# Four interleaved attention layers on one core: where rows are normalised, buffers for prepared weights, places of transpositions, and slots for the rest of a second pass

## The chip, the cores and the metric

The kernel runs on one core of a Trainium2 chip. The metric is the device time of one execution in microseconds. A measurement is the median of some runs; one further execution is recorded by the hardware profiler.

## What is computed

Four layers follow each other over 2048 tokens of width 512, in float32: A, B, A, B, with the same weights in both rounds. Each adds to its input what it makes of the normalised input. A is a linear attention with a learned feature map (two softmaxes per head), B an attention within four segments of 512 tokens with a memory carried from segment to segment. There are 32 heads of 16.

```python
def _layernorm(x, axis=-1, eps=1e-5):
    m = jnp.mean(x, axis=axis, keepdims=True)
    v = jnp.var(x, axis=axis, keepdims=True)
    return (x - m) / jnp.sqrt(v + eps)
...
        pq = jnp.einsum("bhsd,hdf->bhsf", q, w_phi)
        pk = jnp.einsum("bhsd,hdf->bhsf", k, w_phi)
        phi_q = jnp.concatenate([_softmax(pq, axis=-1), _softmax(-pq, axis=-1)], axis=-1)
        phi_k = jnp.concatenate([_softmax(pk, axis=-1), _softmax(-pk, axis=-1)], axis=-1)
        kv = jnp.einsum("bhsf,bhsd->bhfd", phi_k, v)
        z  = jnp.einsum("bhsf->bhf", phi_k)
        num = jnp.einsum("bhqf,bhfd->bhqd", phi_q, kv)
        den = jnp.einsum("bhqf,bhf->bhq", phi_q, z)[..., None] + 1e-6
        o = num / den
...
            logits = jnp.einsum("bhqd,bhkd->bhqk", qs, ks) * scale + mask
            p = _softmax(logits, axis=-1)
            a_dot = jnp.einsum("bhqk,bhkd->bhqd", p, vs)
            pq = phi(qs)
            num = jnp.einsum("bhld,bhde->bhle", pq, M)
            den = jnp.einsum("bhld,bhd->bhl", pq, z)[..., None] + 1e-6
            a_mem = num / den
            o = g * a_mem + (1.0 - g) * a_dot
...
    x = A_x
    x = x + _A_ref(_layernorm(x, axis=-1), A_wqkv, A_w_phi, A_wo)
    x = x + _B_ref(_layernorm(x, axis=-1), B_wq, B_wk, B_wv, B_wo, B_beta)
    x = x + _A_ref(_layernorm(x, axis=-1), A_wqkv, A_w_phi, A_wo)
    x = x + _B_ref(_layernorm(x, axis=-1), B_wq, B_wk, B_wv, B_wo, B_beta)
```

## The kernel before

**Order.** The kernel is a set of Python generators. Each step of a generator issues a few instructions, and the program takes steps from several of them in a fixed order. The wrappers `held` (for TensorE) and `Ordered` (for VectorE, ScalarE, GpSimd and SyncE) tie each instruction to the one issued before it on its engine, so every engine works in exactly the order in which the steps are taken. Instructions of `prepare` are `loose`: they come after their predecessor, but nothing is tied to them. All loads and stores but one kind go over SyncE's queue, which waits at each for its buffer or its data.

**Buffers.** `T2(tag, n)` gives a tile of a ring of n buffers; a new tile of a tag waits until the one n places back is read for the last time. Products that aren't attention use PSUM tiles `g`, a ring of three. Matrix products in high precision take three matmuls per block (`mm3`): high by high, high by low, low by high, so a value is split into a rounded high part (ScalarE) and the rest (VectorE's subtraction): `oh`/`ol`, `hh`/`hl`, the pairs in `w8` and `e8`.

**Normalising rows** (`norm_T`, L409) takes 15 steps: load of four tiles of rows; moments of tiles 0, 1, 2; moments of tile 3 and `guard`; `root` on ScalarE; `refine` (six small instructions, on GpSimd where `off` is set); `normal` four times on ScalarE; `columns` four times, each four transpositions into `g`, a copy to the high part and a subtraction for the low part.

**The linear layer, first pass** (`pass1`, L654) goes over chunks of 512 rows in the order 1, 2, 3, 0. In a chunk, `go` projects k and q in the order k0 k1 q0 q1 k2, then kv(0), k3 q2 q3, each projection in four steps; with kv(1) of the chunk before (`late`, behind k1) these are 36 steps. kv(0) needs the scaled features `es` of k0 and k1. Beside them run, by a plan of steps: the four `columns` of the next chunk (4 to 7), its values `vt` (from 10), and the norm of the chunk after that (8 to 34). The layer in the second round starts differently. Its first chunk is normalised and its values are made while the attention layer before it ends: that layer's table gives steps to it as `begin`, `N`, `n`, `ln` and `v` (L1157 to L1275). In that table, `LAST`, its last twelve value steps, the load of awk among them, stand from slot 6.1 on, and four steps of its k0 in 7.3 and 7.4. The last of the attention layer (`early`, `end`) takes four more. Its second chunk's rows are loaded at step 0 of the first, their moments held in `aside` to the very end of the attention layer, and their columns come at steps 17 to 20.

**The linear layer, second pass** (`pass2`, L826) takes 16 tiles of q features through transpositions, products with KN, weighing, `turn` and the output projection, nine steps each. A20 = 105 of its steps run alone beside `opening` (L1142) of the attention layer, which loads weights, starts the buffers and normalises the layer's first segment (`norm0`). The rest is `side` of `steps` (L1157).

**The attention layer** (`steps`) runs in slots: k from -25 to 163, five for each of 32 blocks m; "slot 6.3" is the third slot of the sixth block of a segment. Up to -10 only projections and the second segment's norm stand there (`BEFORE`); from -9 on `maxima` of block 0 and onward run, each with TensorE's product and VectorE's maxima. `side` is spread over the slots from MAXIMA = -9 to 1, by TensorE work in ns, LEFT = 25000 in all. In the last segment, `early` begins to load its four rows `tb` in slot 5.4 and projects in 7.1, 7.3 and 7.4; `a3`, the memory of the last column block, has its second half in 6.3.

**Preparing weights** (`prepare`, L300) runs beside the first round's first pass. It reads 20 blocks of rows of b_wq, b_wk, a_wo, b_wv and b_wo into `xr` (three buffers, asked for up to three ahead), splits each into `oh` (ScalarE) and `ol` (GpSimd; three buffers each), the first eight in quarters and the last twelve whole, and stores both. One piece moves on every two steps of the pass.

Of the kernel before, what the change touches and what calls it, by code (L numbers as in the profile page):

```python
# [8 lines left out]
F32R = mybir.dt.float32r  # L9
# [17 lines left out]
OT = 6  # L27
TA = 8
OO = 3
# [5 lines left out]
LEAD = 9  # L35
FINAT = 8
PAUSE, DONE = object(), object()
LEFT = 25000
BEGIN = -25
MAXIMA = -9  # L40
A20 = 105
PREP = 3
EVERY = 2
NEXT = (3, 2, 3, 2)
SEGS = (1, 2, 3, 0)
# [60 lines left out]
def interleave_kernel(ctx, tc, x_in, a_wqkv, a_wphi, a_wo, b_wq, b_wk, b_wv, b_wo, b_beta,  # L106
# [15 lines left out]
    def nm(s):  # L122
        uid[0] += 1
        return f"{s}_{uid[0]}"

    def T2(tag, bufs, dt=F32, shape=(P, 512)):
        return sp.tile(list(shape), dt, tag=tag, bufs=bufs, name=nm(tag))
# [8 lines left out]
    aside = [None]  # L136
# [86 lines left out]
    def dtile(shape, name):  # L223
        return dr.tile(list(shape), F32, name=name)
# [75 lines left out]
    def prepare():  # L300


        yield from constants()
        for _ in range(PREP):
            yield
        jobs = [(src, kc) for src in (b_wq, b_wk, a_wo, b_wv, b_wo) for kc in range(NC)]
        asked = []

        def rows():

            while jobs and len(asked) < 3:
                src, kc = jobs.pop(0)
                asked.append(T2("xr", 3))
                sync.dma_start(out=asked[-1], in_=src[kc * P : (kc + 1) * P, :])
            return asked.pop(0)

        def parts():
            return rows(), T2("oh", OO, F32R), T2("ol", OO, F32R)

        def pieces():  # L320
            for m in range(2):
                for kc in range(NC):
                    tiles = parts()
                    for e in range(2):
                        for r in range(2):
                            views = [tiles[0].rearrange("p (c f r e d) -> p e r c d f", c=NC, f=2, r=2, e=2)]
                            views += [t.rearrange("p (c f e d r) -> p e r c d f", c=NC, e=2, f=2, r=2)
                                      for t in tiles[1:]]
                            keep = [wqk[m][:, :, a, kc, :] for a in range(2)] if e and r else ()
                            yield [v[:, e, r] for v in views], keep, tiles[1:]  # L330
            for key in ("awo", "bwv", "bwo"):
                kept[key] = [dtile((P, NC, D), nm(key)) for _ in range(2)]
                for kc in range(NC):
                    tiles = parts()
                    yield tiles, [k[:, kc, :] for k in kept[key]], tiles[1:]

        def turn_by_turn():
            loose[0] = True
            piece = next(todo, None)
            loose[0] = False  # L340
            return piece

        copied, stored, todo = None, None, pieces()
        for piece in chain(iter(turn_by_turn, None), (None, None)):
            loose[0] = True
            if stored:
                _, keep, tiles = stored
                for k, t in zip(keep, tiles):
                    dma(k, t.rearrange("p (c x) -> p c x", c=NC) if len(k.shape) == 3 else t)
            if copied:  # L350
                (raw, hi, lo), _, _ = copied
                pool.tensor_tensor(out=lo, in0=raw, in1=hi.bitcast(F32), op=SUB)
            if piece:
                (raw, hi, _), _, _ = piece
                act.copy(hi, raw)
            loose[0] = False
            copied, stored = piece, copied
            for _ in range(EVERY):
                yield
# [166 lines left out]
    def chain(*gens):  # L526
        for g in gens:
            yield from g
# [56 lines left out]
    class LayerA:  # L585
# [68 lines left out]
        def pass1(self, first):  # L654
            hTs, vv = [], []

            def upcoming(n):

                h = []
                spare = ("e8" if first else "w8") if n % 2 else None  # L660
                return h, norm_T(self.xsrc, SEGS[n], h, spare, slow=True, off=True)

            if first:
                wq, wk, wv, upc = self.first(hTs, vv, upcoming)
            else:
                norm = norm_T(self.xsrc, SEGS[0], hTs, slow=True, off=True)
                for _ in range(11):
                    next(norm)
                    yield
                wv = load_w("awv")  # L670
                for _ in norm:
                    yield
                vt = v_tile(hTs, wv, vv, ("g", G))
                for _ in range(8):
                    next(vt)
                    yield
                wk = load_w("awk", None, "e8")
                yield from vt
            self.mmq = [T2("mmq", 2, shape=(P, NT // 2, 2, H)) for _ in range(2)]
            kva = sp.tile([P, 8, 4 * VW], F32, tag="acc", bufs=1, name=nm("kva"))  # L680
            late = None
            for n, s in enumerate(SEGS):
# [53 lines left out]
                    yield  # L736

                if n < NSEG - 1:
                    if n == 0 and not first:
                        upc = upcoming(1)  # L740
                        next(upc[1])
                    hTs, g = upc
                    vv = []
                    if n or first:
                        plan = [(4 + j, g) for j in range(4)]
                        vals, norms = [10 + j * 26 // 16 for j in range(16)], (8, 14, 16, 18, 20, 22, 24, 28, 30, 32, 34)
                    else:
                        plan = [(j, g) for j in (8, 9, 12, 13, 14, 15, 17, 18, 19, 20)]
                        vals, norms = [21 + j * 13 // 16 for j in range(16)], (21, 26, 27, 28, 29, 30, 31, 33, 34, 35, 36)
                    vt = v_tile(hTs, wv, vv, ("g", G))  # L750
                    plan += [(j, vt) for j in vals]
                    if n + 2 < NSEG:
                        upc = upcoming(n + 2)
                        plan += [(j, upc[1]) for j in norms]
                    plan.sort(key=lambda x: x[0])
                    e = {}

                    def go(late):

                        ready, done = [], []  # L760
                        for step in "k0 k1 q0 q1 k2 v0 k3 q2 q3".split():
                            if step == "v0":
                                yield from kv(0)
                                continue
                            t = int(step[1])
                            yield from (kproj if step[0] == "k" else qproj)(t, e)
                            if done:
                                es.append(scale_k(e[done.pop()]))
                            if ready:
                                exp(e[ready[0]])  # L770
                                done.append(ready.pop())
                            if step[0] == "k":
                                ready.append(t)
                            if step == "k1" and late:
                                yield from late

                    for i, _ in enumerate(go(late)):
                        if i == 4 and n == 0 and not first:
                            wq = load_w("awq", None, "e8")
                            aside[0].append(lambda: [next(g) for _ in range(4)])  # L780
                        while plan and plan[0][0] <= i:
                            next(plan.pop(0)[1], None)
                        if n == 1 and i % 4 == 0:
                            settle(1)
                        yield
                    for _, step in plan:
                        next(step, None)
                    late = kv(1)
                    continue
# [80 lines left out]
    class LayerB:  # L870
# [286 lines left out]
        def steps(self, side, after, table_end):  # L1157
# [67 lines left out]
            for s in range(NSEG):  # L1225
                for cell in (FIRST if s == 0 else GAPS if s < NSEG - 1 else table_end).replace("|", "\n").split("\n"):
                    if cell.strip():
                        at_, *what = cell.split()
                        m, j = at_.split(".")
                        table[8 * R * s + R * int(m) + int(j)] = what, s  # L1230
            slots = list(range(MAXIMA, 2))
            spent = 0.0
            for k in range(BEGIN, R * N + 4):
# [17 lines left out]
                if k in slots:  # L1251
                    want = LEFT * (1 + slots.index(k)) / len(slots) if k < slots[-1] else 1e9
                    while spent + 100 < want:
# [39 lines left out]
    for i in range(2):  # L1293
        lb = LayerB(xs[2 * i + 1], xs[2 * i + 2])
        run(p1[i])
        a2 = la[i].pass2()
        opening = lb.opening()
        for k in range(A20):
            next(a2)
            if k in (6, 9, 12, 18, 24, 30) or k > 41 and k % 3 == 0:  # L1300
                next(opening, None)
        for _ in opening:
            pass
        lb.steps(a2, p1[1] if i == 0 else iter(()), FINAL if i else LAST)
# [31 lines left out]
```

## Time and profile before

| | us |
|---|---|
| median of 3 runs | 1599.54 (1596.8 to 1601.78) |
| profiled execution, its own time | 1604.31 |
| its span, first to last instruction | 1602.6 |
| TensorE busy (matmul) | 1518.1 |
| VectorE busy | 1130.9 |
| ScalarE busy | 785.6 |
| GpSimd busy | 651.7 |
| mean granted TensorE clock | 0.983 of full speed |

The stages in the span: the first round's first pass to about 207 us, its second pass to 283, the attention layer to about 822, then the same again, with the second round's attention from about 1071 to the end. Names of engines in the profile: PE is TensorE (PEld its weight loads), DVE VectorE, ACT ScalarE, POOL GpSimd, SP SyncE's queue. Nearly all lines carry the number of a helper (L161, L183, L187), so groups are told apart by their tiles. The page's line of the granted clock, in 40 slices of 40 us, in tenths of full speed:

```profile
PEclk9998999999999999999988999999999999999999
```

Only three stretches show at this scale: near 140, and from 800 to 880. Finer windows are read below.

### The profile page before, as it was taken

To read this page: it belongs to the slowest core of one execution; us is meant where nothing else is said; L and a number is where in the kernel's file an instruction comes from. 1 tells how busy PE (TensorE), PEld (TensorE's weight loads), DVE (VectorE), ACT (ScalarE), POOL (GpSimd) and SP (SyncE) were. 2 spreads that over 40 slices of the span, in tenths; PEclk is the share of its full clock that TensorE was granted. 3 is DMA by queue.
4 is the path that set the end of the run, shared out by engine and by line. 5 is a ranking of instruction groups with operands and counts; after the bars stand their busy time and mean duration, and the time that the engine had idled before them with its cause. 6 is when DMAs were issued, how large, how long until landed. Compare 5 with 4: busy or idle time off the path is not lost.

```text
span 1602.6 us, 28186 instructions
## 1 busy us (share of the span) xinstructions
PE 1518.1 (95%) x9856; PEld 1083.3 (68%) x9856; DVE 1130.9 (71%) x3252; ACT 785.6 (49%) x1178; POOL 651.7 (41%) x1006
## 2 busy tenths in 40 slices
PE   7998999988999999999989999998989999999997
PEld 6787887765566666665557888877556666666554
DVE  5654677577778878878554557756788788787783
ACT  5543345325565565565533323343455655655553
POOL 1567555213444544433222336532234444433322
PEclk9998999999999999999988999999999999999999
DMA  4477265534443543535231103735353444444331
GB/s 161 135 260 256 66 198 158 157 99 134 126 112 104 143 99 105 142 94 152 90 129 40 40 20 101 235 105 147 111 170 110 107 136 103 106 112 101 80 102 39
DMA packets 108765, 195.71 MB, mean 122 GB/s; under 512 B 14416, under 2 KB 27856, under 8 KB 107856
## 3 DMA queue, kind: packets, MB, share of 16 engines
q1 hardware_dynamic: 107472, 193.38, 41.2%
q8 instruction: 79, 1.29, 0.4%
q10 hardware_dynamic: 1152, 0.52, 0.1%
q14 instruction: 62, 0.51, 0.1%
HBM read 101.05 MB, written 39.85 MB: 88 GB/s over the span
## 4 chain that ended last, share of the span: by engine, by line
PE 67%; DVE 18%; ACT 5%; issue 5%; POOL 3%; DMA 2%; SPq 0%; ACTq 0%; POOLq 0%; DVEq 0%
PE g L183 38%; DVE mx L161 8%; PE lg L183 8%; PE mx L183 8%; PE g L187 7%; PE pv L183 7%; POOL P L161 2%; ACT tb L161 2%; DVE es L161 2%; ACT P L161 1%; DVE mxs L161 1%; DVE ta L161 1%; DVE mmq L161 1%; ACT x L161 1%; DMA xr<-in 1%
## 5 line engine op out<-in xcount | busy, mean ns | idle before, releaser
L161 DVE CUSTOM_DVE_ANT_0 mx<-mx,mask 128x128 f32<-128x128 f32 (+3 forms) x1024 | 510.9, 499 | 163.2 <-PE mx L183 128.6
L161 ACT ACTIVATE P<-lg 128x1024 f32<-128x1024 f32 x320 | 328.8, 1028 | 178.9 <-PE lg L183 171.1
L161 POOL TENSOR_SCALAR_AFFINE_SELECT P<-P 128x256 f32<-128x256 f32 (+1 forms) x448 | 191.3, 442 | 444.3 <-ACT P L161 443.2
L183 PE MATMUL g<-hh,wqk 128*128 128x512 f32 x512 | 180.3, 407 | 1.0 <-ACT mt L161 0.7
L183 PE MATMUL mx<-e,e 63*128 63x256 f32 (+2 forms) x1024 | 156.2, 362 | 25.8 <-DVE mxs L161 20.2
L183 PE MATMUL lg<-e,e 64*128 64x256 f32 (+2 forms) x1024 | 168.5, 387 | 7.9 <-ACT P L161 7.1
L183 PE MATMUL g<-w,oh 128*128 128x512 f32 x512 | 171.5, 417 | 4.3 <-DVE hl L161 2.5
L183 PE MATMUL pv<-P,v 128*32 128x512 f32 (+3 forms) x2048 | 166.1, 443 | 0.0
L183 PEld LDWEIGHTS lg<-e,e 64*128 64x128 f32 x1024 | 81.2, 184 | 102.7 <-issue 53.9
L183 PE MATMUL g<-w,hh 128*128 128x512 f32 x448 | 145.5, 406 | 1.5 <-ACT tb L161 0.9
L161 DVE DVE_READ_ACCUMULATOR2_ANT mxs<- 128x1 f32 x1024 | 144.8, 141 | 0.0
L183 PEld LDWEIGHTS mx<-e,e 63*128 63x128 f32 x1024 | 83.2, 186 | 74.8 <-DVE mxs L161 55.9
L183 PEld LDWEIGHTS pv<-P,v 128*32 128x32 f32 x2048 | 54.0, 110 | 99.6 <-issue 89.2
L183 PEld LDWEIGHTS g<-hh,wqk 128*128 128x128 f32 x512 | 96.3, 188 | 22.3 <-ACT mt L161 1.1
L183 PEld LDWEIGHTS g<-w,oh 128*128 128x128 f32 x512 | 90.9, 192 | 27.3 <-issue 2.8
L161 POOL TENSOR_SCALAR tb<-tb 128x512 f32<-128x512 f32 x48 | 71.5, 1491 | 82.0 <-ACT tb L161 82.0
L183 PE MATMUL g<-w,ol 128*128 128x512 f32 x256 | 103.0, 402 | 0.0
L183 PE MATMUL g<-hl,wqk 128*128 128x512 f32 x256 | 100.0, 390 | 0.0
L161 ACT COPY v<-g 128x512 f32<-128x512 f32 x64 | 37.6, 587 | 120.1 <-PE g L183 119.8
L161 ACT CAST ta<-g 128x512 fp32r<-128x512 f32 x64 | 37.5, 585 | 117.4 <-PE g L183 117.4
L183 PEld LDWEIGHTS g<-w,hh 128*128 128x128 f32 x448 | 79.8, 189 | 20.3 <-ACT tb L161 2.7
L183 PE MATMUL g<-w,hl 128*128 128x512 f32 x224 | 88.1, 393 | 0.0
(133 smaller groups left out, 2729.5 us busy)
## 6 DMA issues: line engine op xcount, KB each, us to landing
e<-ta SPq DMA_DIRECT2D x384, 128.0 KB
wqk<-wqk SPq DMA_DIRECT2D x64, 512.0 KB
x<-x SPq DMA_DIRECT2D x48, 256.0 KB
xr<-in SPq DMA_DIRECT2D x28, 256.0 KB
pq<-tb SPq DMA_DIRECT2D x24, 256.0 KB
tb<-pq SPq DMA_DIRECT2D x24, 256.0 KB
x<-xr SPq DMA_DIRECT2D x24, 256.0 KB
xr<-x SPq DMA_DIRECT2D x24, 256.0 KB
```

The costliest lines, as they stand in the source:

```text
L161: i = f(*a, **k)
L183: return held(nc.tensor.matmul(*a, **k))
L187: return held(nc.tensor.transpose(*a))
```

## The change

- `STEPS` replaces the rule by which `opening` takes its steps during the second pass. The count stays 27; the last four, the columns of `norm0`, move from 93, 96, 99 and 102 to 93, 100, 102 and 109. A20 becomes 110.
- `side` starts at slot -14 instead of -9, with 21700 ns instead of 25000 over 16 slots instead of 11.
- `prepare` takes its rows from the six buffers `ot`, up to five asked ahead, and its parts from the eight buffers `ta1`, two for each piece. Both tags are otherwise used only later, by the second pass and the attention layer.
- In the first pass, columns of the next chunk stand at steps 4, 7, 10 and 13, and the norm after it at 14, 20, 22, 24, 26 (load, moments), 27, 28 (root, refine), 31, 33, 34 and 35.
- In the second round, the second chunk's rows are loaded directly behind awk (slot 6.1), and each of the first chunk's last six value steps (slots 6.3, 6.4, 7.1) is followed by a step of their norm: moments twice, twice, then root and refine, this refine on VectorE. The first chunk's plan holds the four `normal` at 0, 2, 4, 4 and the columns at 8, 9, 11, 13, and its values and next norm follow the plan of the other chunks. The steps held in `aside` are gone.

```diff
-LEFT = 25000
+LEFT = 21700
 BEGIN = -25
-MAXIMA = -9
-A20 = 105
+MAXIMA = -14
+STEPS = (6, 9, 12, 18, 24, 30, *range(42, 91, 3), 93, 100, 102, 109)
+A20 = 110
...
-            while jobs and len(asked) < 3:
+            while jobs and len(asked) < 5:
                 src, kc = jobs.pop(0)
-                asked.append(T2("xr", 3))
+                asked.append(T2("ot", OT))
...
-            return rows(), T2("oh", OO, F32R), T2("ol", OO, F32R)
+            return rows(), T2("ta1", TA, F32R), T2("ta1", TA, F32R)
...
-            def upcoming(n):
+            def upcoming(n, off=True):
...
-                return h, norm_T(self.xsrc, SEGS[n], h, spare, slow=True, off=True)
+                return h, norm_T(self.xsrc, SEGS[n], h, spare, slow=True, off=off)
...
                 wk = load_w("awk", None, "e8")
-                yield from vt
+                upc = upcoming(1, False)
+                next(upc[1])
+                for n, _ in enumerate(vt):
+                    if n > 1:
+                        next(upc[1])
+                    yield
...
-                    if n == 0 and not first:
-                        upc = upcoming(1)
-                        next(upc[1])
                     hTs, g = upc
                     vv = []
-                    if n or first:
-                        plan = [(4 + j, g) for j in range(4)]
-                        vals, norms = [10 + j * 26 // 16 for j in range(16)], (8, 14, 16, 18, 20, 22, 24, 28, 30, 32, 34)
-                    else:
-                        plan = [(j, g) for j in (8, 9, 12, 13, 14, 15, 17, 18, 19, 20)]
-                        vals, norms = [21 + j * 13 // 16 for j in range(16)], (21, 26, 27, 28, 29, 30, 31, 33, 34, 35, 36)
+                    plan = [(j, g) for j in ((0, 2, 4, 4, 8, 9, 11, 13) if n == 0 and not first else (4, 7, 10, 13))]
+                    vals, norms = [10 + j * 26 // 16 for j in range(16)], (14, 20, 22, 24, 26, 27, 28, 31, 33, 34, 35)
...
                         if i == 4 and n == 0 and not first:
                             wq = load_w("awq", None, "e8")
-                            aside[0].append(lambda: [next(g) for _ in range(4)])
...
-            if k in (6, 9, 12, 18, 24, 30) or k > 41 and k % 3 == 0:
+            if k in STEPS:
                 next(opening, None)
```

## The prediction

> **What bounds the kernel now.** I read the page's head first, then a table of windows of 5 us over the whole span, then the timelines of PE, ACT, DVE and SP around the windows that stood out, and the chain of waits there.
>
> ```profile
> PE 1518.1 (95%) x9856; PEld 1083.3 (68%) x9856; DVE 1130.9 (71%) x3252; ACT 785.6 (49%) x1178; POOL 651.7 (41%) x1006
> ```
>
> TensorE is busy for 95% of the span, and no edit takes a matmul away. So the change can only win or lose idle time of PE (84 us in all) and time in which PE is busy at a lower granted clock. The table of windows shows where both sit (columns: window, its length, busy time of PE, PEld, DVE, ACT and POOL with counts, granted clock, DMA share, GB/s):
>
> ```profile
> 150.00:155.00 5.00, 3.52 (x17) 3.52 (x17) 1.69 (x3) 1.24 (x2) 5.00 (x5) 0.50 0.92 344
> 155.00:160.00 5.00, 5.00 (x20) 4.61 (x20) 0.72 (x1) 0.00 (x0) 2.14 (x2) 0.50 0.42 161
> ...
> 310.00:315.00 5.00, 4.63 (x16) 3.44 (x14) 4.64 (x12) 0.60 (x1) 2.82 (x3) 0.66 0.02 3
> 320.00:325.00 5.00, 2.98 (x12) 1.93 (x11) 4.68 (x17) 0.00 (x0) 1.06 (x1) 0.91 0.40 82
> ...
> 830.00:835.00 5.00, 0.88 (x6) 0.85 (x5) 3.09 (x5) 2.77 (x4) 3.88 (x9) 0.77 0.14 52
> 835.00:840.00 5.00, 3.95 (x12) 2.31 (x10) 3.21 (x5) 2.76 (x5) 0.14 (x1) 0.50 0.45 154
> 840.00:845.00 5.00, 3.91 (x19) 3.91 (x20) 3.51 (x6) 1.07 (x2) 2.08 (x2) 0.50 0.22 55
> 845.00:850.00 5.00, 5.00 (x24) 4.92 (x24) 0.96 (x2) 0.59 (x1) 1.67 (x4) 0.50 0.22 52
> 850.00:855.00 5.00, 5.00 (x17) 3.95 (x16) 0.65 (x2) 0.00 (x0) 0.00 (x0) 0.68 0.00 0
> ```
>
> An idle stretch is paid twice: itself, and in the windows behind it at half the clock. The PE timeline names the waits (idle time and what ended it, in brackets):
>
> ```profile
> 127.12 0.65 PE L187 MATMUL g<-ident,x 128*128 128x128 f32 x4 [1.56 <-DVE e L161]
> 142.07 0.73 PE L183 MATMUL g<-w,hh 128*128 128x512 f32 x2 [0.57 <-ACT v L161]
> 151.48 6.67 PE L183 MATMUL lg<-v,P 128*128 128x68 f32 x30 [4.09 <-POOL P L161]
> ...
> 834.16 1.11 PE L187 MATMUL g<-ident,x 128*128 128x128 f32 x4 [4.12 <-ACT x L161]
> 836.74 1.12 PE L187 MATMUL g<-ident,x 128*128 128x128 f32 x4 [0.19 <-ACT tb L161]
> 841.09 1.12 PE L187 MATMUL g<-ident,x 128*128 128x128 f32 x4 [1.96 <-DVE w L161]
> ```
>
> **1. Preparing the weights (-8).** The wait at 151.48 goes back over POOL's P, DVE's es and ACT's copy tb to one ACT instruction:
>
> ```profile
> 145.64 0.62 ACT L161 CAST oh<-xr 128x512 fp32r<-128x512 f32 x1 [3.62 <-DMA bwv<-ol]
> ```
>
> ACT waited 3.62 us until a pair of oh/ol (three pairs) had been stored, and five times (9.5 us) for xr, loaded at most three rows ahead. The change makes this five rows ahead and four pairs. In the stretch of whole rows (120.4 to 152.6) a piece took 2.9 us; two steps of the first pass without stalls are 2.3 us, so one more pair gives a store 2.3 us more and two more rows give a load 4.6 us more, against waits of at most 3.6 and 2.9 us. Removable: 1.56 + 0.57 + 4.09 = 6.2 us idle and half of the 8.5 us busy at 0.50, 4.3 us, together 10.5. Against it: DMA must move 12 x 0.79 MB in about 26 us, 360 GB/s. DMA ran at 382 GB/s over the window 80 to 100 us, so this is near the limit, not beyond it. I take 8; bounds 0 and 10.5. The Trainium skill (DMA: Bandwidth & Descriptors, Specifications) puts the HBM limit of a core at about 358 GB/s; the 382 measured here is above it. By the page a part of the wait would stay, and the term would be nearer 5.
>
> **2. Norm steps later in the first pass (-1.5).** Moments of the next rows now stand at steps 20 to 26 instead of 14 to 18, behind the es chain that kv(0) waits for. Two moments are 2 x 0.80 us of DVE (BN stats 0.61, aggregate 0.18). PE's gaps before kv(0) are 0.79 (at 102.4), 0.68 (at 899.8) and 0.96 (columns, at 923.9). Bounds 0 and 3; I take 1.5.
>
> **3. Columns of norm0 moved inside the second pass (-2).** At 272 to 280 and at 1062 to 1067 PE waits for hl and P behind transpositions that fell between phT and turn: 1.35 and 1.4 us. At the new steps 100 and 109 they stand among the output projection. Bounds 0 and 3.
>
> **4. The second pass's rest (-4).** Five steps go ahead of the attention layer's loop, and 21.7 us of PE work is spread over 16 slots (1.36 each) instead of 25 over 11 (2.27). Lost now in 305 to 335: 4.2 us idle and 3.1 us of clock; in 1095 to 1120: 3.8 and 3.0. DVE is 94% busy at 310 to 325 (maxima, es, tmp, ol in one queue) and about 40% at 290 to 310, so work moved ahead finds DVE free. But ACT is late there: the layer's rows reach BN stats only at 300.06, root follows at 301.22, and ACT then works without pause to 310.5. Steps of the second pass at slot -13 (PE about 299) put their copies behind root. So part of the wait only moves. I take 2 of 7 per layer; bounds -14 and +20 for both (rival C).
>
> **5. Second linear layer's start: gain (-15).** Moments, root, refine and two normals go into the last half chunks, the rest runs before the columns, and aside no longer holds four moments in front of k1's features (824.87 to 828.36). Removable: idle 4.12 + 0.19 + 1.96, clock 8.2 (busy time of the five windows from 830 on, times one minus clock), and two gaps of 0.97 and 1.59 at 876 to 880 that end with the same squeezed norm: 17.1 us. What is late next is k1's es: DVE from 823.8 has about 13 us of extremes, hl, mmq and es, then POOL 1.5, so kv(0) can start near 838 where PE, without waits, arrives at 837. That leaves 1 to 2 us: 15. Bounds 10 and 17.
>
> **6. Second linear layer's start: price (+13.9).** This part may surprise. The rows are still asked for behind the load of awk, and SP's queue shows when that goes out:
>
> ```profile
> 768.62 23.25 SPq L161 DMA_DIRECT2D tb<-x  x4
> 791.92 3.83 SPq L161 DMA_DIRECT2D e<-awk  x8
> 795.84 2.46 SPq L161 DMA_DIRECT2D x<-x  x4
> ```
>
> The last tb waits 21.5 us for a matmul of the memory (its buffer); awk is 2.1 MB, the rows 1 MB more, and DMA falls silent at 804.5. The last 1 MB ran at about 400 GB/s, so rows land from about 802 to 804.5. Before, moments came at 824.87 and waited for nothing. Now moments 0 and 1 are issued in slot 6.3, where DVE's next instruction (r<-g of the memory) stood at 791.52. Queued behind them on DVE: that weighing, whose PSUM buffer g is the one that early's first projection needs (three rotate), then ol of turn (794.38). PE reaches that projection at 795.86 and needs ol for its third matmul. With row 3 at 804.5, moment 0.8, guard 0.2 and ol 0.6, ol is there at about 806: PE stands 9.6 us. ACT's root and refine stand behind the same rows. Behind the 4.09 us gap at 147 to 151 PE was at half clock for 8.5 us, so add 4.3: 13.9. Bounds: 0 if rows landed before; 18 with the 8.2 us of clock behind 834. The Trainium skill (TensorE: Matmul & The Clock Gate, Part 1) lets the full clock return after one busy window of some 3.4 us. That would be 1.7 us, and the term 11.3. The rows here show 8.5 us and more, and I go by them.
>
> Refine on DVE instead of POOL: six small instructions, 1.4 us on POOL (831.17 to 832.56), hidden under the same stall; uncovered it would add at most 1.4.
>
> **Sum.** -8 - 1.5 - 2 - 4 - 15 + 13.9 = -16.6 us. The profiled execution took 1604.31 (span 1602.6 and 1.7 around it) and would take 1587.7; it stands 4.8 above the median 1599.54, from which the forecast is **1583**. Taking the terms as partly independent, its own range is 1574 to 1592.
>
> **Rivals.**
> A. *The handover does not stall*: rows land early enough or nothing PE needs stands behind the moments. For: PE has 25 us of other work there. Against: its order is fixed, and early's projection is next. 1583 - 13.9 = **1569**.
> B. *The wait for weights stays*, since transfers and not buffers set it (DMA share 0.76 to 0.98 from 125 to 140). Against: 382 GB/s elsewhere. Term 1 falls to -1: **1590**.
> C. *Slower: the moved second-pass work is paid twice.* In slots -14 to -10 PE meets copies behind ACT's late root; it stands about 5 us (299 to 304) and loses 4.3 at half clock, 9.3 per layer; the stage from 306 on gets no shorter, DVE setting its pace, +0.7 of moved copies. Term 4 becomes +20: **1607**. It decides as soon as these slots lose more than 6 us per layer. For: row 300.06 and ACT's unbroken work behind it. Against: PE still has q1, k1 and v3 (8 us) to lay between.
> D. *Nothing to be seen*: term 6 with the long clock (18), term 1 at -1, term 4 at 0: -16.6 + 4.1 + 7 + 4 = -1.5: **1598**.
>
> **How the numbers follow.** Forecast 0.52, A 0.12, B 0.14, C 0.11, D 0.11. A measurement of this kernel tells about 0.3%, 4.8 us, from no change. Faster: 0.52 + 0.12 + 0.14 = 0.78; same 0.11; slower 0.11. The range 1567 to 1599 takes in A, B and D and leaves out C and what lies below A.
>
> **What would show it.** Step 1: no idle over 2 us at 120 to 152, clock 1.00 at 150 to 160, ACT's oh without DMA waits. Step 3: no wait for hl near 275. Step 4: less idle between maxima of the first two blocks; a gap at slot -13 would be C. Step 5: no idle of 4 us ahead of the second linear layer's columns. Step 6: DVE's BN stats waiting about 11 us for DMA x near 790, and PE idle near 796 with a low clock behind; if that is missing, A. The prediction is wrong if the stall of step 6 is over 25 us or the gap at 151 stays.

## The result, and the profile after

The changed kernel takes 1611.67 us (median of 11 runs, 1604.97 to 1620.44) against 1601.78 before (11 runs, 1596.8 to 1604.25). The ratio is 1.0064 with an interval of 1.0044 to 1.0085: some 10 us slower, where 17 us faster was forecast. The profiled execution took 1609.61 (span 1607.9).

The page's first line after shows the same work:

```profile
PE 1520.0 (95%) x9856; PEld 1080.0 (67%) x9856; DVE 1131.2 (70%) x3258; ACT 785.4 (49%) x1178; POOL 649.5 (40%) x1000
```

So again only idle time and granted clock can differ. To place them I cut the span where certain instructions of PE come for the first time: KN (second pass begins), the first matmul with mem and tb (the attention layer's second segment), the last of these in the round. For each piece the windows give the idle time of PE and the time lost to a clock below 1 (busy time times one minus clock). What is left over is the same in all kernels to within some 2 us.

| stage, profiled executions: length (idle, lost to clock), us | before | after |
|---|---|---|
| first pass, round 1 (start to KN) | 208.1 (19.4, 4.4) | 203.7 (14.4, 3.4) |
| second pass and opening, round 1 (KN to mem) | 221.9 (14.9, 3.4) | 224.6 (16.1, 4.4) |
| attention, round 1 (to last mem) | 360.9 (7.1, 1.5) | 359.5 (7.2, 0.0) |
| handover and first pass, round 2 (to KN) | 205.5 (12.1, 8.4) | 212.0 (18.7, 8.1) |
| second pass and opening, round 2 (KN to mem) | 221.7 (14.7, 3.4) | 223.3 (16.7, 2.9) |

The first pass won 4.4 us. The handover lost 6.5, and both openings lost where a gain was forecast. The five stages differ by 5.0 us in sum: the execution profiled before took longer than its kernel's median and the one after less than its own, so the table places only half of the 10 us.

PE's timeline after, with idle time and releaser in brackets:

```profile
128.38 4.48 PE L184 MATMUL mx<-v,P 128*128 128x68 f32 x30 [1.34 <-POOL P L162]
151.17 3.56 PE L184 MATMUL lg<-v,P 128*128 128x68 f32 x30 [0.33 <-POOL P L162]
...
318.09 0.50 PE L184 MATMUL mx<-e,e 63*128 63x512 f32 x2 [0.79 <-DVE mxs L162]
322.11 0.90 PE L184 MATMUL mx<-e,e 63*128 63x256 f32 x4 [1.59 <-DVE mxs L162]
325.36 0.80 PE L184 MATMUL mx<-e,e 63*128 63x256 f32 x4 [0.77 <-DVE mxs L162]
...
803.16 1.22 PE L184 MATMUL g<-w,oh 128*128 128x512 f32 x2 [10.27 <-DVE tmp L162]
805.43 0.79 PE L184 MATMUL g<-w,ol 128*128 128x512 f32 x1 [1.05 <-DVE ol L162]
840.18 1.14 PE L184 MATMUL g<-w,w 128*128 128x512 f32 x3 [2.95 <-DVE w L162]
```

In the same place of the opening the kernel before has one wait for DVE's maxima over half a microsecond:

```profile
322.82 0.50 PE L183 MATMUL mx<-e,e 63*128 63x512 f32 x2 [2.02 <-DVE mxs L161]
```

The 4.09 us ahead of kv(0) are 0.33 now, and the 4.12 us ahead of the columns are gone (2.95 remain behind them). In their place PE stands 11.3 us in the middle of the handover. The cause of this last wait, in the timelines of SP, DVE and ACT after:

```profile
788.51 0.32 SPq L162 DMA_DIRECT2D tb<-x  x1
788.88 3.88 SPq L162 DMA_DIRECT2D e<-awk  x8
792.80 3.59 SPq L162 DMA_DIRECT2D x<-x  x4
```

```profile
800.60 0.69 DVE L162 BATCH_NORM_STATS2 bs<-x 128x6 f32<-128x512 f32 x1 [13.18 <-DMA x<-x]
...
804.83 0.55 DVE L162 TENSOR_TENSOR ol<-g,oh 128x384 fp32r<-128x384 f32 x1
```

```profile
804.96 0.45 ACT L162 ACTIVATE st<-st 128x4 f32<-128x4 f32 x2 [10.94 <-DVE st L162]
```

The rows stand behind awk, which stands behind the last tb. DVE waits 13.18 us for them and everything behind its moments waits too, ol last.

### The profile page after: what moved, and what is told of

Read it like the earlier page. It is cut to its first block, busy times and chain, and to the rows that moved or that the text cites. A ratio compares the mean times of both kernels' runs of the same rounds, so it can differ in the third digit from the quotient of the medians.

```text
span 1607.9 us, 28179 instructions
## 1 busy us (share of the span) xinstructions
PE 1520.0 (95%) x9856; PEld 1080.0 (67%) x9856; DVE 1131.2 (70%) x3258; ACT 785.4 (49%) x1178; POOL 649.5 (40%) x1000
## 4 chain that ended last, share of the span: by engine, by line
PE 67%; DVE 17%; ACT 5%; issue 4%; POOL 3%; DMA 3%; SPq 1%; ACTq 0%; POOLq 0%; DVEq 0%
PE g L184 38%; DVE mx L162 8%; PE mx L184 8%; PE lg L184 8%; PE pv L184 7%; PE g L188 7%; POOL P L162 2%; DVE es L162 2%; ACT tb L162 1%; ACT P L162 1%; DVE mxs L162 1%; DMA x<-x 1%; DVE ta L162 1%; SPq L162 1%; DVE mmq L162 1%
```

## The experiments

All are the kernel before or after with few lines changed, each timed in five rounds beside the kernel before. Microseconds in the text are a ratio less one, times 1601.

| kernel | ratio to before | interval | us |
|---|---|---|---|
| prep_only | 0.9961 | 0.9947 to 0.9975 | -6.2 |
| start_only | 1.0015 | 0.9996 to 1.0033 | +2.4 |
| opening_only | 1.0045 | 1.0030 to 1.0060 | +7.2 |
| spacing_only | 1.0017 | 0.9995 to 1.0038 | +2.7 |
| slots_only | 1.0150 | 1.0134 to 1.0165 | +24.0 |
| steps_only | 0.9993 | 0.9983 to 1.0002 | -1.1 |
| load_first | 0.9984 | 0.9965 to 1.0003 | -2.6 |
| slots_load_first | 1.0058 | 1.0035 to 1.0081 | +9.3 |
| opening_load_first | 1.0022 | 1.0005 to 1.0038 | +3.5 |
| ahead_thick | 0.9980 | 0.9968 to 0.9991 | -3.2 |
| rows_early | 0.9959 | 0.9947 to 0.9972 | -6.6 |
| both_rows | 0.9947 | 0.9931 to 0.9962 | -8.5 |
| prep_start_rows_early | 0.9893 | 0.9879 to 0.9906 | -17.1 |
| prep_start_steps | 0.9857 | 0.9831 to 0.9884 | -22.9 |
| best_load_first | 0.9853 | 0.9835 to 0.9871 | -23.5 |

**The change in four parts.** Theory H held that the handover's stall makes the change slow, theory O that the opening of the attention layers does, theory N that neither part matters and only the clock's draw differs.

Each takes its lines of the change's diff and leaves the rest as before: prep_only the three lines of `prepare`; start_only `upcoming` with `off`, its steps in `vt`, the first chunk's plan and the end of `aside`; opening_only the constants at the top and `if k in STEPS`; spacing_only the two lists of the other chunks:

```diff
-                        plan = [(4 + j, g) for j in range(4)]
-                        vals, norms = [10 + j * 26 // 16 for j in range(16)], (8, 14, 16, 18, 20, 22, 24, 28, 30, 32, 34)
+                        plan = [(j, g) for j in (4, 7, 10, 13)]
+                        vals, norms = [10 + j * 26 // 16 for j in range(16)], (14, 20, 22, 24, 26, 27, 28, 31, 33, 34, 35)
```

> The kernel before with one part of the change: rows from ot, five asked ahead, parts from ta1. Theory H (the handover to the second linear layer makes the change slow: DVE and ACT wait about 11 us for rows that stand behind awk in SP's queue; the other parts give or take a few us): -4 to -5 us, as the second pass starts 4.4 us earlier in the profile after (203.70 against 208.12), PE's wait of 4.09 us for POOL's P near 151 gone. Theory O (the opening of the attention layers makes it slow): the same -4 to -5. Theory N (the parts do nothing; the granted clock is drawn anew): within 2 us of before.

> The kernel before with one part of the change: the second round's start of the linear layer (rows loaded behind awk, moments, root and refine in the last half chunks, refine on VectorE, the first chunk's new plan). Theory H: +7 us (from +6 to +10), with BN stats waiting 10 us or more for DMA x in the trace near 800 and PE idle 10 us there; the gap of 4.12 us ahead of the columns gone. Theory O: between -3 and +2, the stall being paid back whole by the gap that goes. Theory N: within 2 us.

> The kernel before with one part of the change: STEPS, A20 = 110, LEFT = 21700, MAXIMA = -14. Theory H: +2 to +5 us (the trace after shows 2.7 us lost in the first opening and 1.6 in the second). Theory O: +8 or more. Theory N: within 2 us.

> The kernel before with one part of the change: columns at 4, 7, 10, 13 and norm at 14 to 35 in all chunks but the second round's first. Theory H and theory O: 0 to -2 us, gaps of PE before kv(0) in the first pass shorter. Theory N: within 2 us. The four single parts should add up to the whole change's +10 us if they don't act on each other.

prep_only gave 6.2 us, near H and O, not N. In its trace ACT's waits for loads are gone and some for stores are left, hidden from PE (ACT's copies, then PE's kv(0)):

```profile
134.69 0.62 ACT L161 CAST ta<-ot 128x512 fp32r<-128x512 f32 x1 [1.92 <-DMA awo<-ta]
137.54 0.62 ACT L161 CAST ta<-ot 128x512 fp32r<-128x512 f32 x1 [2.23 <-DMA awo<-ta]
...
145.14 0.62 ACT L161 CAST ta<-ot 128x512 fp32r<-128x512 f32 x1 [2.58 <-DMA bwv<-ta]
```

```profile
147.39 3.56 PE L183 MATMUL lg<-v,P 128*128 128x68 f32 x30 [0.42 <-POOL P L161]
```

ACT still waits 7.4 us for stores in this stretch, yet PE stands 0.42 us where it stood 4.09. start_only's interval (-0.6 to +5.3) reaches into O's range and stops short of H's, though its trace has the stall that H names (PE stands 9.81 us at 803.29); opening_only is just under O's 8: neither theory alone. spacing_only's interval holds both no change and a loss of 6 us. Its twelve times fall in two groups of six, 1597 to 1603 and 1609 to 1612, and the trace is of the first group. There the gap before kv(0) at 102 shrank from 0.79 to 0.38, and a new one of 1.34 came before kv(1), as in the changed kernel's line at 128.38. Its sign stays open. But its trace shows something on the first part too, since its buffers are those of the kernel before:

```profile
151.91 3.56 PE L183 MATMUL lg<-v,P 128*128 128x68 f32 x30 [0.33 <-POOL P L161]
```

The wait of 4.09 us ahead of this kv(0) is gone here as well. So either part alone takes it away, and a sum of the parts counts it twice. By the profiles, the first round's first pass took 208.1 us before, 199.9 in prep_only, 204.4 in spacing_only and 203.7 with both. The four parts sum to +6.1, the whole is +10.2, with some 3 us of uncertainty on each.

**The handover.** Ask for the rows ahead of tb and awk in SP's queue, and move nothing else:

```diff
-                for _ in range(8):
+                for j in range(8):
+                    if j == 6:
+                        upc = upcoming(1, False)
+                        next(upc[1])
                     next(vt)
                     yield
                 wk = load_w("awk", None, "e8")
-                upc = upcoming(1, False)
-                next(upc[1])
```

> The changed kernel, but the second chunk's rows are asked for at slot 5.3, ahead of the four tb and of awk in SP's queue; the moments stay in slots 6.3 and 6.4. If the wait of DVE for those rows is the price of the handover (theory H): no BN stats wait over 1 us and no PE idle of 10 us near 795, and about 11 to 14 us faster than the changed kernel, so 4 us faster to 2 slower than before. If that wait only moved idle time that PE would have had elsewhere (theory O): within 4 us of the changed kernel, +6 to +10 against before.

> The kernel before with the weights' buffers and the second round's start of the change, its rows asked for at slot 5.3; opening and spacing as before. Theory H: prep's -6 and, without the stall, -8 to -14 for the start, together -14 to -20 us, 1582 to 1588. Theory O: -6 to -8.

rows_early turned the whole change from +10.2 to -6.6 us. Its SP and DVE timelines:

```profile
765.92 2.01 SPq L162 DMA_DIRECT2D x<-x  x4
768.03 19.83 SPq L162 DMA_DIRECT2D tb<-x  x4
787.92 4.69 SPq L162 DMA_DIRECT2D e<-awk  x8
```

```profile
786.37 0.68 DVE L162 BATCH_NORM_STATS2 bs<-x 128x6 f32<-128x512 f32 x1
```

The same three loads in another order: the rows go out at 765.92 instead of 792.80, and the moments start with no wait shown. The stage from the last mem to KN is 194.3 us (7.3 idle, 1.7 lost to clock) against 212.0. Theory H holds for the handover.

**The opening.** Its two halves apart. Theory S: the thinner filling beside the maxima (less of the second pass's rest per slot) costs it; theory C: the new places of the columns do.

```diff
-MAXIMA = -9
+MAXIMA = -14
```

is slots_only; steps_only is the opening part without this line.

> The kernel before with MAXIMA = -14 alone: the same 25 us of the second pass's rest over 16 slots, A20 and the opening's steps as before. Theory S (the thinner filling beside the maxima, from slot -9 on, leaves PE waiting for DVE's mxs and brings the lower clock): +4 to +7 us, most of the +7 of the whole opening part, with waits for DVE mxs and granted clock under 0.8 at about 315 to 330. Theory C (the new places of the columns inside the second pass cost it): 0 to +2.

> The kernel before with STEPS, A20 = 110 and LEFT = 21700, but MAXIMA = -9: the rest of the second pass over the same 11 slots, 1.97 us each. Theory S: 0 to +2 us. Theory C: +4 to +7 us, with PE waiting for hl, hh and tmp at the new steps.

The columns' new places cost nothing (theory C falls), and the spreading alone costs 24 us, more than three times what S expected. So S is too small a story for slots_only. Each of its openings has 7 to 8 us more idle and 4 us more lost to clock. PE, DVE and ACT in the first:

```profile
302.82 0.80 PE L183 MATMUL g<-hh,wqk 128*128 128x512 f32 x1 [3.01 <-DVE ol L161]
...
316.32 0.66 PE L187 MATMUL g<-ident,tmp 128*128 128x128 f32 x4 [1.65 <-ACT tb L161]
```

```profile
296.62 0.69 DVE L161 BATCH_NORM_STATS2 bs<-x 128x6 f32<-128x512 f32 x1 [3.09 <-DMA x<-x]
```

```profile
301.12 0.45 ACT L161 ACTIVATE st<-st 128x4 f32<-128x4 f32 x2 [2.85 <-DVE st L161]
```

Again rows that land late: here the attention layer's second segment, loaded behind wqk. DVE's moments wait for them, ACT's root waits for the moments, the second pass's turn stands behind root, and PE waits for its ol. That is theory R, tried by moving this load ahead of wqk:

```diff
-BEFORE = {-25: "q0", -23: "v0", -21: "k0", -20: "load", -19: "v1",
+BEFORE = {-25: "load q0", -23: "v0", -21: "k0", -19: "v1",
```

> Control: the kernel before, with the load of the attention layer's second segment of rows moved from slot -20 to slot -25, ahead of q0 and of the load of wqk that q0 asks for in SP's queue. Theory R (those rows, late behind wqk, hold DVE and ACT, and so what stands behind them): 0 to -3 us. Theory S (the thinner filling beside the maxima): within 2 us.

> MAXIMA = -14 alone, which made it 25 us slower, now with the rows' load at slot -25. Theory R: PE's wait of 3.0 us for turn's ol at 302.8 and the half clock behind it go, and it is at most 10 us slower than before. Theory S: still +20 us or more, as the filling beside the maxima is as thin.

> The opening part of the change (STEPS, A20 = 110, LEFT = 21700, MAXIMA = -14), which made it 7 us slower, now with the rows' load at slot -25. Theory R: within 2 us of before or faster. Theory S: +5 to +8 us, with the waits for DVE mxs of 1.6 and 0.8 us near 326 to 330 still there.

With the rows early, slots_only falls from +24.0 to +9.3. PE's wait of 3.01 at 302.82 is gone, that for tb is not: R holds for the larger part of what slots_only lost.

For the change's own opening R isn't shown. That part falls from +7.2 to +3.5, but the intervals (+4.8 to +9.6 and +0.8 to +6.1) overlap, +3.5 lies between the ranges of R and S, and PE's waits in the traces are the same with the rows late and early. DVE and ACT do wait for the rows in the changed kernel (2.91 us ahead of the moments at 298.05, 3.23 ahead of root), yet PE is idle for only 0.2 us from 284.4 to 317.2: in this order of steps nothing that PE needs there stands behind them. What it waits for comes later, beside the maxima. Three first lines of PE's waits there (total, times, longest): one that opening_only, opening_load_first and the changed kernel have alike, steps_only's, and that of the kernel before:

```profile
PE mx L184 <- DVE mxs L162: 4.2, 4, 1.6
```

```profile
PE mx L184 <- DVE mxs L162: 2.0, 1, 2.0
```

```profile
PE mx L183 <- DVE mxs L161: 2.0, 1, 2.0
```

opening_only and steps_only differ in MAXIMA alone: 21.7 us of PE work lie over 16 slots, 1.36 each, or over 11, 1.97 each. With the thinner filling PE waits 4.2 us for the maxima instead of 2.0, and the clock is at half beside these waits for 10.2 us (326.0 to 336.3) instead of 3.4 (320.2 to 323.6), both in the first opening. In times, +7.2 stands against -1.1. So in the change it is S.

What remains of slots_load_first's +9.3 could be the thin filling (S) or the place of second-pass steps between the projections (P). ahead_thick (MAXIMA = -14 and the load at slot -25) has steps there and keeps the filling thick:

```diff
-                    want = LEFT * (1 + slots.index(k)) / len(slots) if k < slots[-1] else 1e9
+                    want = (660 * (k + 15) if k < -9 else 3300 + 21700 * (k + 10) / 11) if k < slots[-1] else 1e9
```

> The kernel before with the rows' load at slot -25, A20 = 105, and the second pass's rest as 3.3 us over slots -14 to -10 (0.66 each) and 21.7 us over -9 to 1 (1.97 each). Theory S (thinner filling beside the maxima costs what is left): within 3 us of before. Theory P (the place of second-pass steps among the projections costs it): +5 to +9 us, as in slots_load_first.

It is 3 us faster than before, like load_first alone, so steps between the projections are not dear in themselves. It puts 3.3 us there where slots_load_first puts 7.8, so P at the larger dose isn't excluded.

**Together.** both_rows is the whole change with both loads moved ahead.

> The whole change with both late loads of rows moved ahead (slot 5.3 of the second round's handover, slot -25 of the attention layers). If the two loads are what made it slow: rows_early's -5 and the 4 us that the early load gave the opening, -8 to -10 us against before. If the opening's load has no part in it: -4 to -6.

It is where R and H together expected it, but this doesn't decide for R: rows_early alone is at -6.6, the intervals of the two overlap, and in the openings PE's waits for the maxima are alike in both traces. Moving the two loads is worth 10.2 + 8.5 = 18.7 us to the whole change; 16.8 of them came with the handover's load, and what the opening's adds isn't shown.

**A version that beats both.** The parts that paid, with one load or both moved.

> A version made of what paid: the weights' buffers, the second round's start with its rows asked for at slot 5.3, and A20 = 110 with the new places of the columns, but the rest of the second pass over the old 11 slots and the old spacing. If the parts add: 1583.7 - 2 = about 1582 us; both theories of the opening expect the same.

> prep_start_steps with the rows' load at slot -25. If the early load's gain adds: 1577 to 1580 us; if the steps move has already taken that wait away: within 2 us of prep_start_steps' 1580.6.

1580.6 and 1577.4 us; the intervals overlap, so what the second load adds isn't shown. Either is some 30 us under the changed kernel and over 20 under the kernel before.

## Why the prediction was wrong, point by point

**The step that failed is the fourth: "work moved ahead finds DVE free", and with it "I take 2 of 7 per layer".** Costed at -4 us, the spreading over 16 slots costs +7.2 together with the third step; steps_only, which has the third step and the five steps moved ahead but the old 11 slots, is at -1.1. The term let the waits beside the maxima shrink; they grew, from 2.0 us in one wait to 4.2 in four (opening_only and the changed kernel), with a longer stretch at half clock beside them. DVE was 94% busy at 310 to 325, as the prediction itself says, and sets the pace there. What PE does between two maxima then only fills its time. With 1.36 us of it per slot PE stands longer than with the 1.97 of steps_only or the 2.27 of the kernel before. The work moved ahead was done without a wait, as forecast (0.2 us idle from 284.4 to 317.2 in the changed kernel); the time it left behind was not saved.

The rival I called C had half of this ("the stage from 306 on gets no shorter, DVE setting its pace"). Its other half, PE standing about 5 us behind root in slots -14 to -10, did not come in the changed kernel. It came in slots_only (3.01 us at 302.82), where other steps fall in these slots. That slots_only's +24.0 lies near C's +20 for this term is luck as far as the change goes, whose opening part lost 7. For slots_only the view that should have weighed more was in my own text: BN stats at 300.06 and root at 301.22. I weighed DVE's 40% load at 290 to 310 against it. But of DVE's idle time there, 3.04 and 1.15 us were waits for these very rows, at the moments from 296.05 on (300.06 is only the fourth of them), and a step placed behind such a wait waits as well. Nor did ACT work "without pause" from root to 310.5: it waited 1.31 us at 303.45 and 0.76 at 305.49. The point at which C was to decide was 6 us per layer: the idle and clock loss of each opening rose by 11 to 12 us in slots_only and by 4 in opening_only.

**The fifth step's size.** The gain of the second round's start, -15, is best read from prep_start_rows_early less prep_only: -17.1 + 6.2 = -10.9 us. What stayed is 2.95 us of waiting for w behind the columns: their high copy stands in ACT's queue behind the exponential of k0's features (837.87), and that waits for POOL's differences (835.76 to 837.8), which start only when the attention layer has ended.

**The sixth step was right.** PE stood 10.27 + 1.05 = 11.3 us where 9.6 was forecast, for the reason given and with SP's order as read. The price, +13.9, measures as start_only less the start without the stall, 2.4 + 10.9 = 13.3 us, or as the whole change less rows_early, 16.8. Of the clock: it stayed at 0.50 from 796.4 to 810.1, so 6.9 us behind PE's return at 803.16 and 4.6 behind its second wait, less than the 8.5 I took. Both are longer than the one busy window of some 3.4 us of the Trainium skill (TensorE: Matmul & The Clock Gate, Part 1), and the term of 11.3 that followed from it is further from 13.3 than mine.

**The first step** was right in kind and a little large: -6.2 of -8, and the gap at 151 fell from 4.09 to 0.42 in prep_only. The same transfers with more buffers took it away, so their rate alone had not set it, as argued against rival B. Nor had the buffers alone: spacing_only kept the old ones and has 0.33 there, which the prediction did not foresee.

**The second and third.** -1.5 and -2 were forecast. steps_only, which holds the third, is at -1.1 with an interval that reaches zero; the wait of 1.23 us for hl at 278.12 is gone in its trace, and waits of 0.69 for tmp and 0.68 for hh stand at 285.02 and 286.32 instead. spacing_only is at +2.7 with an interval that does too; a gap that shrinks in one place came back at kv(1). ACT's first normal now waits 3.25 us there for refine on POOL (117.96 in spacing_only); the copies of q behind it come late, and DVE's reductions of these stand ahead of es.

With measured terms, -6.2 + 2.7 + 7.2 - 10.9 + 13.3 = +6.1, and the whole is +10.2. The missing 4 us are within what the intervals of the parts allow. One place where parts do act on each other is shown: prep_only and spacing_only take away the same wait at 151, and the sum counts it twice. Whether that makes up the 4 us was not settled.

## What to carry to other kernels

Before a step is moved earlier, ask when its data land: follow its load through the queue that issues it, past what stands ahead there, and then list what stands behind the step on its in-order engine. An engine that looks idle in a window may be held by exactly that wait, and is then no room for more work. Moving the load ahead was worth more here (about 13 us in one place, 15 in slots_only) than where the step itself stood. And where one engine sets the pace of a stage, taking work of another engine out of it saved nothing here: it only left longer gaps.

## What the runs showed of the hardware that I had not expected

The clock falls after much less than the 4 us gaps of the profile before. Windows of the changed kernel:

```profile
130.00:135.00 5.00, 5.00 (x26) 4.60 (x26) 1.69 (x3) 1.49 (x2) 5.00 (x5) 0.58 0.67 195
...
320.00:325.00 5.00, 3.00 (x12) 1.71 (x11) 4.75 (x17) 0.00 (x0) 1.05 (x1) 0.70 0.32 71
325.00:330.00 5.00, 4.64 (x15) 3.11 (x16) 2.73 (x11) 0.00 (x0) 0.00 (x0) 0.62 0.00 0
```

At 130.8 it fell behind a gap of 1.34 us that stands ahead of matmuls only 68 columns wide (another, of 1.01, lies 5 us before it); at 322.0 at the end of a gap of 1.59 with one of 0.79 four us before it. In the kernel before it fell at 310.4 behind gaps of 0.77 and 0.37, and at 324.1 behind one of 2.02. The low stretches named here, read in windows of half a microsecond, last 6.8 us at 131, 6.8 at 322, 13.7 at 796 and 3.4 at 841, and in the kernel before 10.2 at 150, 3.4 at 310, 3.4 at 324 and 20.5 at 833: 1, 2, 3, 4 and 6 times 3.4 us.

Whether such a short gap brings the clock down isn't stable. both_rows has the same gaps of 0.99 and 1.33 in its first pass and no low stretch behind them. The first opening (KN to mem) is the same in the kernel before, prep_only and spacing_only; it lost 3.4 us to the clock in the profile of the first and none in those of the others. So single executions of kernels that agree in a stage differ by 3 us there, and parts worth less than that need the interval and not one profile.
